# A state-space kernel with an MLP behind it: order of the first loads, of the first differences and of the second weights' decoding

## The chip, the cores and the metric

One Trainium2 chip, one core of it. The metric is device microseconds (us) of one execution, lower is better. A core has a matmul engine (PE), three engines for everything else on chip data (VectorE = DVE, ScalarE = ACT, GpSimd = POOL), a queue processor (SP) that issues DMAs, and 16 DMA engines. Each engine runs its own list of instructions in order and waits on semaphores that others raise; ACT can issue DMAs from its list too (its queue is written ACTq, SP's is SPq).

## The reference, cut to what matters

Two blocks, the second fed by the first. Shapes: 4 batches, 8 heads, 768 steps, head size 32, state size 16.

```python
# block 1, per batch and head, in chunks of the sequence
log_a = np.log(np.clip(a, 1e-6, 1.0)); cum = np.cumsum(log_a of the chunk)
L  = np.exp(cum[:, None] - cum[None, :]) * causal
y  = ((C @ B.T) * L) @ x  +  (C @ state) * np.exp(cum)[:, None]
state = np.exp(cum[-1]) * state + (B * np.exp(cum[-1] - cum)[:, None]).T @ x
# block 2, on 3072 rows (batch x step) of 256 (head x size)
h = y @ w_in                       # 256 -> 2048
g = h * np.clip(h + 3, 0, 6) / 6
out = g @ w_out                    # 2048 -> 256
```

`w_in` and `w_out` come as float64. The kernel takes each weight's halves apart with integer operations and puts a float32 together ("decoding").

## The kernel before, in words

The 768 steps are cut into 6 chunks (c = 0 to 5) of 128 steps. A chunk first gets its block-1 output y, for all 32 pairs of batch and head, and then runs through the MLP as k = c: 16 slices f of the hidden size, each with a matmul into PSUM (`mlp_in` for k = 0), a ramp on ACT (`ramp`, L796) and a product on DVE (`times_ramp`, L801). While the MLP of chunk k runs on PE, the other engines prepare chunk k + 1. The order of all instructions on each engine is the order in which the Python calls them: it is written out by hand at the end of the function. Only chunk 0 has no MLP to hide behind. What follows is its path, which the change rebuilds.

**Loads.** SP issues, in this order: `a` (L83), C of chunk 0 in eight pieces (`pairs_first`, L103, one per batch and half of the heads, 128 rows of 256 bytes each), x (`load_x`, L121, 4096 runs of 128 bytes) and the weight pieces 1 to 3 (`load_w`, L144, 1 MB each). ACT issues weight piece 0 (L144) and B (L96, 4096 runs of 64 bytes), and only then loads its function table (L150). The framework gives the DMAs eight semaphores in turn; a DMA whose semaphore is still in use by an earlier one waits at the head of its queue until that one has landed. By the built program the sixth C piece waits for weight piece 0 in this way, the seventh for `a`, the eighth for the first C piece.

**Decays.** DVE and ACT make log a and its running sum (`log_a` L284 and L286, `add_up` L289), `in_three` (L296 to L300) splits it into three bf16 parts. PE makes the differences cum[i] - cum[j] in a PSUM bank: a mask (`diff_mask`, L370, and `mask_again`, L378), minus the row's sum (`diff_less`, L383, one matmul of 512 columns), plus the column's sum (`diff_pick`). The last has two forms: sixteen narrow matmuls, one per head and half (L399), for batches 0 and 1 of half c = 0; for the rest two matmuls of 512 columns (L391) from a table that DVE spreads by head beforehand (`spread_rows`, L279). `diff_exp` (L407) takes the exponential on ACT into L. Thirty matmuls of one column (L365) stand among the masks. The index c = 0 or 1 here means chunk 0 or 1: both chunks' differences are made in front.

**Scores and output of chunk 0.** `turn_b` turns B with PE (L464) and copies it to SBUF with ACT (L473). `turn_squares` turns C on DVE (L507), `part_heads` makes two masked copies (L517). `busy` (L535) is two matmuls whose result nobody reads. `scores` (L572) makes C times B in four banks; inside it, `into_state` (L590) makes the two half-chunk sums for the state, from x and from B times L's last column (`ends`, on POOL, L438). `multiply` copies one sum (`take`, L606), scales the other (L616) and multiplies L by the scores, pair of heads by pair (L621). `mix` (L667 with `from_state`, L545) makes y, `keep` (L683) copies it to `yT`.

**Weights.** `decode(i)` is a Python generator; `weights(i, n)` advances it n steps, and each step puts a few instructions on ACT (a copy of the top halfword L202, two ramps L227 and L230) and on DVE (L207, L211, L221, L223, L234, L244). Pieces 0 to 3 are w_in, each serves four slices f; pieces 4 to 7 are w_out. Three raw buffers go round. `load_w` of piece 2 is held back by a one-element memset on DVE (L143), since SP must wait for it. Piece 1 is decoded between `mix` and the first slice of the MLP, pieces 2 to 5 are woven into the loop over f (dictionary `weave`). `renew(0)`, which makes the state after chunk 0 (L642, L600), is called behind that loop, among the first products with w_out (`first_out`, L814).

Of the kernel before, what the change touches and what calls it, by code (L numbers as in the profile page):

```python
# [8 lines left out]
FP32 = mybir.dt.float32  # L9
# [12 lines left out]
def kernel(  # L22
# [65 lines left out]
    def load_bc(c):  # L88

        sl = slice(c * P, (c + 1) * P)

        def tokens_first(src, queue=nc.sync, **where):
            t = loads.tile([P, NB * NH, N], FP32, **where)
            queue.dma_start(out=t, in_=src[:, :, sl, :].rearrange("b h s n -> s (b h) n"))  # L96
            return t

        def pairs_first(src):
            t = loads.tile([P, 2, NB, 4, N], FP32, name="pairs", tag="bc")  # L100
            for b in range(NB):
                for h in range(2):
                    nc.sync.dma_start(  # L103
                        out=t[:, h, b].rearrange("s a n -> s (a n)"),
                        in_=src[b, h:NH:2, sl, :].rearrange("h (s a) n -> h s (a n)", a=4))
            return t

        if 0 < c < TURN:
            bcs[c] = [tokens_first(C, name="C", tag="bc")]
        Bs[c] = tokens_first(B, nc.scalar if c == 0 else nc.sync, name="B", bufs=1)  # L110
        if c == 0:
            bcs[c] = [pairs_first(C), Bs[c]]
# [17 lines left out]
    def load_w(i, queue=nc.sync):  # L130
# [57 lines left out]
    parity = const.tile([P, 2], FP32, name="parity")  # L188

    def decode(i):  # L190

# [8 lines left out]
        m = att.tile([P, n], U32, name="wm")  # L200
        for sl in (slice(0, n),) if i != 1 else (slice(0, n // 2), slice(n // 2, n)):
            nc.scalar.copy(out=s[:, sl], in_=top[:, sl])  # L202
            if i == 1 and sl.start == 0:
                yield

# [11 lines left out]
        if i == 0:  # L217
            next(parts_m)
            next(parts_m)
        yield  # L220
# [3 lines left out]
            out=s, in0=s, scalar1=0x8000, scalar2=None, op0=ALU.bitwise_and)  # L224
        next(parts_m, None)
        yield
# [3 lines left out]
        nc.scalar.activation(e, e.bitcast(BF16), AF.Relu, bias=bias_lo, scale=-1.0)  # L230
        if i and i + NRAW < 2 * NP:
            load_w(i + NRAW)
# [21 lines left out]
    low = pre[:G, 10, :2 * P]  # L254
    spread = [pre[:, 11 + c].bitcast(BF16).rearrange("k (h i) -> k h i", h=NH) for c in range(2)]
    of_batch = const.tile([P, NB], BF16, name="of_batch")
    of_head = const.tile([P, NH], BF16, name="of_head")

# [3 lines left out]
    def row_signs():  # L262
        with nc.allow_low_precision("zeros and ones"):
            nc.vector.tensor_reduce(
                out=pick, in_=ident[:, :pad].rearrange("g (r q) -> g q r", r=3), axis=AX.X,
                op=ALU.add)
            nc.vector.tensor_reduce(
                out=of_batch, in_=pick.rearrange("k (b h) -> k b h", b=NB), axis=AX.X, op=ALU.add)
            nc.vector.tensor_reduce(
                out=of_head, in_=pick.rearrange("k (b h) -> k h b", b=NB), axis=AX.X, op=ALU.add)  # L270
        nc.scalar.mul(less, pick, -1.0)
# [3 lines left out]
            out=parity, in_=head.rearrange("p q t -> p t q"), axis=AX.X, op=ALU.add)  # L275

    def spread_rows(c):

        nc.vector.tensor_tensor(  # L279
            out=spread[c], in0=split[:, c].unsqueeze(1).to_broadcast([P, NH, P]),  # L280
            in1=of_head.unsqueeze(2).to_broadcast([P, NH, P]), op=ALU.mult)

# [72 lines left out]
    def diff_mask(c, b):  # L355
# [5 lines left out]
        else:  # L361
            d = ps_y.tile([P, NH, HT], FP32, name="d", tag=f"y{b % 2}")
        if (c, b) == (0, NB - 1):
            for _ in range(30):
                nc.tensor.matmul(  # L365
                    out=d[:1, 0, :1], lhsT=ident_h[:, :1], rhs=hide[:, :1], start=True, stop=True,
                    skip_group_check=True)
        n = NH // 4
        for h in range(0, NH, n):
# [18 lines left out]
    def diff_pick(c, b):  # L388
        if c or b >= 2:
            for a, rows in enumerate(HALF):  # L390
                nc.tensor.matmul(  # L391
                    out=ds[c, b][rows], lhsT=of_batch[:, b:b + 1].to_broadcast([P, HT]),
                    rhs=spread[c][:, :, rows], start=False, stop=True,
                    tile_position=(0, a * HT), skip_group_check=True)
            return
        for h in range(NH):
# [134 lines left out]

    def busy(n, bank):

        for _ in range(n):
            nc.tensor.matmul(  # L535
                out=bank[:, :256], lhsT=ident,
                rhs=ident.unsqueeze(1).to_broadcast([P, 2, P]), start=True, stop=True)

    def from_state(c, a, pairs=range(NQ)):
# [18 lines left out]
    def scores(c):  # L558
# [6 lines left out]
        cbs[c] = [ps.tile([P, NB, 2, HT], FP32, name="cb", tag=f"f{q}") for q in range(NQ)]  # L565
        if c not in ys:
            own_banks(c)
# [8 lines left out]
        if c == TURN:  # L576
            from_state(c, 0)
        if c <= TURN:
            into_state(c, *range(1 if c == TURN else 2))
# [28 lines left out]
    def multiply(c):  # L608
# [579 lines left out]
    for k in range(NC):  # L1188
        gTs[k] = ffn.tile([P, NF, TB], FP32, name="gT")
        c, ahead = k + 1, k + 2  # L1190
        if k == 0:
# [20 lines left out]
            for i in range(NP):  # L1212
                for b in range(NB):
                    first_out(b, i, c)
                    for n in w_more.get((i, b), ()):
                        next(ins[n])
                    if (i, b) == (1, 0):
                        renew(0)
                    if (i, b) == (1, 1):
# [167 lines left out]
```

## Time and profile before

| | |
|---|---|
| time, median of 3 runs (lowest to highest) | 337.47 us (336.9 to 337.77) |
| the profiled execution's own time | 337.3 us |
| its span in the profile | 335.6 us |
| PE busy in the span | 98% |
| DVE, ACT, POOL busy | 79%, 62%, 39% |
| first matmul of the MLP (L693) starts | 21.73 us |
| the 16 slices of k = 0 end on PE | 49.55 us |

The span is the time from the first to the last recorded instruction; 1.7 us of the execution's own time lie around it. A row of a timeline gives start, time taken, engine, line, operation, output <- input, shapes and count; in square brackets stands the idle time of the engine ahead of it and what ended that. The chain of waits is followed back from the last instruction; a piece of it named "issue" is time in which the engine waited for nothing that the profile shows. The table of windows gives, for each stretch, the busy time of each engine with its count of instructions, the clock that the throttle granted to PE, the mean busy share of the DMA engines (it can pass 1) and the bytes moved.

### The profile page before, as it was taken

To read this page: it belongs to the slowest core of one execution; us is meant where nothing else is said; L and a number is where in the kernel's file an instruction comes from. 1 tells how busy PE (TensorE), PEld (TensorE's weight loads), DVE (VectorE), ACT (ScalarE), POOL (GpSimd) and SP (SyncE) were. 2 spreads that over 40 slices of the span, in tenths; PEclk is the share of its full clock that TensorE was granted. 3 is DMA by queue.
4 is the path that set the end of the run, shared out by engine and by line. 5 is a ranking of instruction groups with operands and counts; after the bars stand their busy time and mean duration, and the time that the engine had idled before them with its cause. 6 is when DMAs were issued, how large, how long until landed. Compare 5 with 4: busy or idle time off the path is not lost.

```text
span 335.6 us, 8329 instructions
## 1 busy us (share of the span) xinstructions
PE 327.6 (98%) x3361; PEld 272.8 (81%) x3361; DVE 264.2 (79%) x418; ACT 208.2 (62%) x448; POOL 130.3 (39%) x125
## 2 busy tenths in 40 slices
PE   7989999999999999999999999999999999999995
PEld 5554888888888888887888888888888888899995
DVE  6879999879599639869949558938678958599973
ACT  4778887657987570677662577643487221677661
POOL 2200000280743896089973078771058740000000
PEclk9999999999999999999999999999999999999999
DMA  8979960684930214239107258100151001210001
GB/s 174 158 275 212 215 237 9 154 107 126 197 37 4 60 48 109 41 51 96 42 2 163 35 76 77 33 4 11 28 75 14 2 4 17 29 20 0 2 0 63
DMA packets 90181, 25.22 MB, mean 75 GB/s; under 512 B 82784, under 2 KB 86528, under 8 KB 89632
## 3 DMA queue, kind: packets, MB, share of 16 engines
q1 hardware_dynamic: 85760, 23.39, 36.9%
q10 hardware_dynamic: 4384, 1.31, 1.8%
q8 instruction: 26, 0.43, 0.5%
q14 instruction: 11, 0.09, 0.1%
HBM read 21.33 MB, written 3.29 MB: 73 GB/s over the span
## 4 chain that ended last, share of the span: by engine, by line
PE 90%; DVE 4%; DMA 3%; issue 1%; SPq 1%; ACT 1%; DVEq 0%
PE h L757 31%; PE wc L1005 8%; PE wb L1005 8%; PE o L814 8%; PE h L693 8%; PE wa L1005 7%; PE o_end L969 6%; PE wb L1013 3%; PE y L667 3%; PE y L545 2%; DVE q_part L897 2%; DMA raw<-in_moe_w_in_dram 2%; PE cb L572 2%; DVE gT L801 1%; DMA pairs<-in_C_dram 1%
## 5 line engine op out<-in xcount | busy, mean ns | idle before, releaser
L801 DVE SCALAR_TENSOR_TENSOR gT<-gT,h 128x512 f32<-128x512 f32 x96 | 64.7, 683 | 22.0 <-ACT gT L796 20.7
L796 ACT ACTIVATE gT<-h,half 128x512 f32<-128x512 f32 x96 | 65.5, 684 | 24.3 <-PE h L757 21.1
L777 ACT ACTIVATE h<-h 128x512 f32<-128x512 f32 x66 | 38.3, 585 | 37.0 <-PE h L757 36.7
L757 PE MATMUL h<-y_hi,w_part 128*128 128x512 f32 x160 | 50.9, 403 | 0.0
L757 PE MATMUL h<-y_less,w_part 128*128 128x512 f32 x160 | 50.1, 399 | 0.0
L757 PE MATMUL h<-y_lo,w_part 128*128 128x512 f32 x160 | 49.5, 395 | 0.0
L860 POOL TENSOR_TENSOR s<-gT 128x512 f32<-128x512 f32 x16 | 25.3, 1582 | 51.5 <-DVE gT L801 51.5
L757 PEld LDWEIGHTS h<-y_lo,w_part 128*128 128x128 f32 x160 | 30.0, 188 | 6.9
L757 PEld LDWEIGHTS h<-y_hi,w_part 128*128 128x128 f32 x160 | 30.1, 188 | 6.7
L757 PEld LDWEIGHTS h<-y_less,w_part 128*128 128x128 f32 x160 | 29.1, 188 | 6.2 <-DVE h L774 0.3
L427 ACT ACTIVATE L<-L,cum_n 128x64 f32<-128x64 f32 x128 | 31.7, 337 | 1.8 <-POOL L L162 1.8
L814 PE MATMUL o<-w_out,gT 128*128 128x256 f32 x128 | 28.8, 381 | 0.0
L693 PE MATMUL h<-yT,w_in 128*128 128x256 f32 (+1 forms) x100 | 27.8, 440 | 0.0
L814 PEld LDWEIGHTS o<-w_out,gT 128*128 128x128 f32 x128 | 24.1, 190 | 3.4
L693 PEld LDWEIGHTS h<-yT,w_in 128*128 128x128 f32 x100 | 18.9, 190 | 8.6 <-issue 5.7
L860 POOL TENSOR_TENSOR gT<-gT 128x512 f32<-128x512 f32 x16 | 23.9, 1500 | 0.7
L897 DVE TENSOR_TENSOR q_part<-gT,q_part 128x256 fp32r<-128x256 f32 x24 | 21.5, 923 | 0.1
L969 PE MATMUL o_end<-v_pair,g_pair 128*128 128x256 f32 x120 | 21.1, 281 | 0.0
L346 POOL TENSOR_SCALAR cum_n<-cum_t 128x128 f32<-128x128 f32 x1 | 0.5, 534 | 51.9 <-DVE cum_t L344 51.9
L162 POOL TENSOR_SCALAR_AFFINE_SELECT L<-L 64x1024 f32<-64x1024 f32 (+1 forms) x16 | 19.2, 1210 | 3.5 <-DMA L<-cum_d 3.1
L860 POOL TENSOR_TENSOR s<-s,gT 128x512 f32<-128x512 f32 x16 | 20.6, 1292 | 0.0
L438 POOL TENSOR_TENSOR bs<-B,L 128x128 f32<-128x128 f32 x24 | 12.1, 528 | 21.7 <-ACT L L427 14.2
(163 smaller groups left out, 636.2 us busy)
## 6 DMA issues: line engine op xcount, KB each, us to landing
raw<-in_moe_w_out_dram SPq DMA_DIRECT2D x4, 1024.0 KB
L<-cum_d SPq DMA_DIRECT2D x8, 512.0 KB
xt<-in_x_dram SPq DMA_DIRECT2D x6, 512.0 KB
raw<-in_moe_w_in_dram SPq DMA_DIRECT2D x3, 1024.0 KB
out_dram<-back SPq DMA_DIRECT2D x128, 16.0 KB
pairs<-in_C_dram SPq DMA_DIRECT2D x40, 32.0 KB
B<-in_B_dram SPq DMA_DIRECT2D x5, 256.0 KB
eto<-cum_e SPq DMA_DIRECT2D x20, 64.0 KB
```

The lines of the kernel that those rows point to most:

```text
L162: nc.gpsimd.affine_select(out=t[rows], in_=t[rows], pattern=pattern, compare_op=ALU.is_ge, fill=-1e5, base=base, channel_multiplier=-1)
L427: nc.scalar.activation(Ls[c][:, b, h], Ls[c][:, b, h], AF.Exp, bias=cum_n[:, c, g:g + 1])
L693: nc.tensor.matmul(out=h[:, t:t + n], lhsT=w_in[f // FP][:, j, f % FP * P:(f % FP + 1) * P], rhs=yTs[k][:, j].rearrange("p b i -> p (b i)" ...
L757: nc.tensor.matmul(out=hs_[k, f], lhsT=w[j][:, f % FP * P:(f % FP + 1) * P], rhs=y[:, j], start=(start and j == 0), stop=True, skip_group_ ...
L777: nc.scalar.activation(h, h, AF.Copy, scale=1.0 / EPS + 1.0)
L796: nc.scalar.activation(gTs[k][:, f], h, AF.Relu, bias=half, scale=1.0 / 6.0)
L801: nc.vector.scalar_tensor_tensor(out=g, in0=g, scalar=1.0, in1=h, op0=ALU.min, op1=ALU.mult)
L814: nc.tensor.matmul(out=o[:, b % 2], lhsT=gTs[0][:, f, b * P:(b + 1) * P], rhs=w_out[:, f], start=(f == 0 and b % 2 == 0), stop=True, skip_ ...
L860: nc.gpsimd.tensor_tensor(out=o, in0=p_, in1=q_, op=op)
L897: nc.vector.tensor_tensor(out=l[:, j], in0=g[:, j], in1=h[:, j].bitcast(FP32), op=ALU.subtract)
L969: nc.tensor.matmul(out=ends_["cross" if n == 2 else "squares"][b], lhsT=g_parts[t][n][:, b * P:(b + 1) * P], rhs=w, start=(t == 0 and b < ...
L1005: nc.tensor.matmul(out=bank[:, slot], lhsT=lhs[:, j], rhs=rhs[:, j], start=(clear and j == 0), stop=True, skip_group_check=True)
```

## The change

- SP's queue: the eight C pieces are cut by head (32 rows by 4 batches of 256 bytes) and not by batch and half of the heads. B follows them on SP, then x. ACT loads its function table first and then issues weight piece 0. By the built program, the seventh C piece waits for `a`, the eighth for the first C piece, and B waits for weight piece 0.
- Weight piece 1 is no longer issued in front. A memset on DVE behind the first product of `multiply(0)` holds it, as another held piece 2 before.
- `spread_rows`, `of_batch`, `of_head` and the wide form of `diff_pick` are gone: every head's difference is made by its own narrow matmuls, for both chunks. The thirty one-column matmuls and `busy` are gone, and the masks are wider (256 or 512 columns and not 128).
- PE's order: differences of chunk 0, those of batch 0 and 1 of chunk 1 around the turning of B, scores, then the differences of batches 2 and 3 of chunk 1 with their exponentials, and only then `into_state`, which has been taken out of `scores`.
- `turn_squares(C)` and `part_heads` move to the front of DVE's list, right behind `in_three`; B's turned copy is made by DVE and not by ACT.
- `decode(0)` takes its second significand step later; `decode(1)` is replaced by `decode_halves(1)`, which runs whole behind `keep(0)`, the exponent part in two halves of the columns. `renew(0)` is called in front of `mix(0)`.
- `mlp_in` runs every matmul 512 columns wide; before, the last 18 of 32 were two of 256.

```diff
-            for b in range(NB):
-                for h in range(2): ... in_=src[b, h:NH:2, sl, :] "h (s a) n -> h s (a n)"
+            if c == 0:
+                for h in range(NH):
+                    rows = slice(h // 2 * 32, h // 2 * 32 + 32)
+                    nc.sync.dma_start(
+                        out=t[rows, h % 2].rearrange("s b a n -> s b (a n)"),
+                        in_=src[:, h, sl, :].rearrange("b (s a) n -> s b (a n)", a=4))
+                return t
...
-        Bs[c] = tokens_first(B, nc.scalar if c == 0 else nc.sync, name="B", bufs=1)
+        Bs[c] = tokens_first(B, name="B", bufs=1)      # behind pairs_first(C)
...
-        if i == 2:
+        if 0 < i < 3:
             nc.vector.memset(raw[:, :1], 0)
...
-    load_w(0, nc.scalar)
-    load_bc(0)
-    load_x(0)
-    load_w(1)
-    nc.scalar.preload_act_table_set("natural_log_exp_and_others")
+    load_bc(0)
+    nc.scalar.preload_act_table_set("natural_log_exp_and_others")
+    load_w(0, nc.scalar)
+    load_x(0)
...
+    def decode_halves(i):
+        for h in halves:
+            nc.scalar.copy(out=s[:, :, h], in_=top[:, :, h])
+        nc.vector.tensor_scalar(out=m, in0=hi, ...)                    # 128x1024
+        for h in halves:
+            for t, mask in ((e, 0x7FF0), (s, 0x8000)):
+                nc.vector.tensor_scalar(out=t[:, :, h], in0=s[:, :, h], ...)
+            nc.scalar.activation(e[:, :, h].bitcast(BF16), e[:, :, h], AF.Relu, ...)
+            nc.scalar.activation(e[:, :, h], e[:, :, h].bitcast(BF16), AF.Relu, ...)
+        nc.vector.scalar_tensor_tensor(out=m.bitcast(FP32), in0=lo, ...)   # 128x1024
+        load_w(i + NRAW)
+        for h in halves:
+            nc.vector.tensor_tensor(out=e[:, :, h], ...)
+            nc.vector.scalar_tensor_tensor(out=w_in[i][:, :, h], ...)
...
-        nc.scalar.copy(out=turned(c)[0], in_=t_ps)
+        (nc.scalar.copy if c else nc.vector.tensor_copy)(out=turned(c)[0], in_=t_ps)
...
+            if c == 0 and q == 0:
+                load_w(1)                              # in multiply
...
-            n = TB // (1 + (f * NK + j >= NF * NK - 18))
+            n = TB // (1 + (f * NK + j >= NF * NK - 0))
...
-    for c in range(2):
-        spread_rows(c)
-    diff(0, 0, 1)
-    diff(0, 2, 3)
+    turn_squares(bcs[0][0], turned(0)[2])
+    part_heads(0)
     weights(0, 1)
+    for b in (0, 2):
+        diff(0, b, b + 1)
     for b in range(NB):
         diff_exp(0, b)
     first_eto()
-    diff(1, 2, 3)
     weights(0, 1)
+    diff(1, 0)
+    turn_b(0)
+    diff(1, 1)
     for b in range(NB):
         ends(0, b)
-    turn_b(0)
-    diff(1, 0, 1)
-    weights(0, 2)
-    diff_exp(1, 2)
-    diff_exp(1, 3)
-    turn_squares(bcs[0][0], turned(0)[2])
-    part_heads(0)
+    weights(0, 1)
+    scores(0)
+    weights(0, 1)
+    for b in range(2, NB):
+        diff(1, b)
+        diff_exp(1, b)
+    own_banks(0)
+    into_state(0, 0, 1)
+    multiply(0)
     fade(0, HALF[1])
     weights(0, 1)
-    busy(2, ps.tile([P, NB * P], FP32, name="d", tag="f3"))
-    scores(0)
-    multiply(0)
+    weights(0, 1)
     load_w(2)
     load_w(3)
-    weights(0, 1)
-    weights(1, 1)
+    renew(0)
     mix(0)
-    keep(0, lambda: weights(1, 1))
-    weights(1, 3)
-    weights(1, 1)
+    keep(0)
+    decode_halves(1)
```

More of the change, by code (lines that the diff above doesn't have):

```diff
@@ L109, in load_bc @@
             bcs[c] = [tokens_first(C, name="C", tag="bc")]
-        Bs[c] = tokens_first(B, nc.scalar if c == 0 else nc.sync, name="B", bufs=1)
         if c == 0:
-            bcs[c] = [pairs_first(C), Bs[c]]
+            bcs[c] = [pairs_first(C)]
+        Bs[c] = tokens_first(B, name="B", bufs=1)
+        if c == 0:
+            bcs[c].append(Bs[c])
         elif c < TURN:
@@ L188 @@
     parity = const.tile([P, 2], FP32, name="parity")
+    def decode_halves(i):
+        n, cut = NK * FP * P, FP * P // 2
+        top = raws[i].bitcast(U16).rearrange("p (k f w) -> p k f w", k=NK, w=4)[..., 3]
+        lo, hi = (raws[i].rearrange("p (n w) -> p n w", w=2)[:, :, w] for w in range(2))
+        s = att.tile([P, n], U16, name="ws").rearrange("p (k f) -> p k f", k=NK)
+        e = att.tile([P, n], U16, name="we").rearrange("p (k f) -> p k f", k=NK)
+        m = att.tile([P, n], U32, name="wm")
+        halves = [slice(h * cut, (h + 1) * cut) for h in range(2)]
+        for h in halves:
+            nc.scalar.copy(out=s[:, :, h], in_=top[:, :, h])
+        nc.vector.tensor_scalar(
+            out=m, in0=hi, scalar1=0xFFFFF, scalar2=0x100000,
+            op0=ALU.bitwise_and, op1=ALU.bitwise_or)
+        for h in halves:
+            for t, mask in ((e, 0x7FF0), (s, 0x8000)):
+                nc.vector.tensor_scalar(
+                    out=t[:, :, h], in0=s[:, :, h], scalar1=mask, scalar2=None,
+                    op0=ALU.bitwise_and)
+            nc.scalar.activation(
+                e[:, :, h].bitcast(BF16), e[:, :, h], AF.Relu, bias=bias_hi, scale=-8.0)
+            nc.scalar.activation(
+                e[:, :, h], e[:, :, h].bitcast(BF16), AF.Relu, bias=bias_lo, scale=-1.0)
+        nc.vector.scalar_tensor_tensor(
+            out=m.bitcast(FP32), in0=lo, scalar=2.0 ** -32, in1=m, op0=ALU.mult, op1=ALU.add)
+        load_w(i + NRAW)
+        m = m.bitcast(FP32).rearrange("p (k f) -> p k f", k=NK)
+        for h in halves:
+            nc.vector.tensor_tensor(
+                out=e[:, :, h], in0=e[:, :, h], in1=s[:, :, h], op=ALU.bitwise_or)
+            nc.vector.scalar_tensor_tensor(
+                out=w_in[i][:, :, h], in0=m[:, :, h], scalar=2.0 ** -20,
+                in1=e[:, :, h].bitcast(BF16), op0=ALU.mult, op1=ALU.mult)
     def decode(i):
@@ L200, in decode @@
         m = att.tile([P, n], U32, name="wm")
[L201 to L204, printed above, removed]
+        nc.scalar.copy(out=s, in_=top)
         def significand():
@@ L218, in decode @@
             next(parts_m)
-            next(parts_m)
         yield
@@ L224, in decode @@
             out=s, in0=s, scalar1=0x8000, scalar2=None, op0=ALU.bitwise_and)
-        next(parts_m, None)
+        if i:
+            next(parts_m)
         yield
@@ L230, in decode @@
         nc.scalar.activation(e, e.bitcast(BF16), AF.Relu, bias=bias_lo, scale=-1.0)
-        if i and i + NRAW < 2 * NP:
+        if i > 1 and i + NRAW < 2 * NP:
             load_w(i + NRAW)
@@ L254 @@
     low = pre[:G, 10, :2 * P]
-    spread = [pre[:, 11 + c].bitcast(BF16).rearrange("k (h i) -> k h i", h=NH) for c in range(2)]
-    of_batch = const.tile([P, NB], BF16, name="of_batch")
-    of_head = const.tile([P, NH], BF16, name="of_head")
     cum_c = cum.rearrange("g (c p) -> g c p", p=P)
@@ L266, in row_signs @@
                 op=ALU.add)
[L267 to L270, printed above, removed]
         nc.scalar.mul(less, pick, -1.0)
@@ L275, in row_signs @@
             out=parity, in_=head.rearrange("p q t -> p t q"), axis=AX.X, op=ALU.add)
[L277 to L281, printed above, removed]
     def log_a(sl):
@@ L362, in diff_mask @@
             d = ps_y.tile([P, NH, HT], FP32, name="d", tag=f"y{b % 2}")
[L363 to L368, printed above, removed]
+        n = NH if c else NH // (2 if b == 0 else 4)
         for h in range(0, NH, n):
@@ L388, in diff_pick @@
     def diff_pick(c, b):
[L389 to L395, printed above, removed]
         for h in range(NH):
@@ L530, in turn_all @@
         fade(c)
[L532 to L537, printed above, removed]
     def from_state(c, a, pairs=range(NQ)):
@@ L565, in scores @@
         cbs[c] = [ps.tile([P, NB, 2, HT], FP32, name="cb", tag=f"f{q}") for q in range(NQ)]
-        if c not in ys:
+        if c not in ys and c:
             own_banks(c)
@@ L577, in scores @@
             from_state(c, 0)
-        if c <= TURN:
+        if 0 < c <= TURN:
             into_state(c, *range(1 if c == TURN else 2))
@@ L1216 @@
                         next(ins[n])
-                    if (i, b) == (1, 0):
-                        renew(0)
                     if (i, b) == (1, 1):
```

## The prediction, made before the changed kernel ran

> **What bounds the kernel now.** I read the chain of waits first. From 21.80 us on it is PE almost without a break: the MLP of chunk 0, then the products with w_out (L814). So a gain must come from an earlier start of that stretch, or from PE needing less inside it. Second, the chain's first 22 us:
>
> ```profile
> 0.79 6.00 DMA raw<-in_moe_w_in_dram
> 6.80 0.71 SPq L103
> ...
> 7.56 1.58 SPq L103
> ...
> 9.18 3.62 DMA pairs<-in_C_dram
> ...
> 12.98 1.12 DVE csT L507
> ...
> 15.16 1.20 PE cb L572 x59
> 16.36 0.84 PE y L590 x50
> ...
> 17.22 0.38 ACT adds L606
> ...
> 17.64 0.90 PE y L667 x55
> ...
> 19.42 1.03 issue
> 20.44 0.75 PE y L667 x43
> ```
>
> The reader sees C arriving last: its sixth piece waits for weight piece 0 to land (6.80), the eighth lands at 12.80. Everything behind is a chain of single steps, with one hole of 1.03 us (19.42) that no semaphore explains. Third, the table of windows:
>
> ```profile
> 4.00:5.00 1.00, 1.00 (x23) 0.97 (x19) 0.83 (x3) 0.66 (x2) 0.00 (x0) 1.00 1.01 393
> 9.00:10.00 1.00, 1.00 (x34) 0.54 (x28) 1.00 (x2) 0.68 (x2) 0.00 (x0) 1.00 0.40 70
> ```
>
> The last two columns say that weight piece 0 moved at 393 GB/s, but that while C is the latest thing the DMA engines were 40% busy at 70 GB/s. The packet records of the trace agree: C's 256-byte packets take 18 ns, some 60 to 90 start per half microsecond, and their times add up to 2 to 4 busy engines of 16. Fourth, the waits of DVE, ACT and PE: from 25.21 to 65 us DVE is never idle, so DVE is the second bound of k = 0.
>
> **Part 1, arrival of C and B.** SP issues a C piece in 0.59 to 0.71 us when nothing holds it, so eight from 1.25 end at about 6.1. Spread evenly, a piece is 8 packets per engine (0.15 us). The record from issue to use of a small load is that of `a`: issued 0.79, used 4.02; the packets of weight pieces start 0.5 to 1.2 us behind the issue. I take C at 8.0 (bounds: 7.3, if the last piece needs only 1.2 us behind its issue; 9.3, if SP is held up as in its 2.14 us piece at 4.55).
>
> [...]
>
> Weight piece 0 goes behind the table load (L150, 1.28 us), so issue near 2.1 and not 0.79. It took 6.0 us from issue to landing beside `a`, whose cold packets held the engines until about 3; with those past I take 4.9, that is 7.0 (5.9 if the DMA isn't held by the table load, 8.0 at the old 6.0). B waits for it on SP: issue 0.5 us, first packet 0.4 us later, 4096 packets in 2.3 us (second B load, packets 32.0 to 34.3), 0.4 us to land: 10.7 (bounds 9.6 and 12.2). Before, B was used at 10.9. x follows: its packets took 4.2 us before (11.0 to 15.3), now 10.4 to 14.5.
>
> **Part 2, from B and C to the MLP.** C's arm on DVE: turn 1.12 and masked copies 0.89, then three decoding steps (L207 0.69, L221 and L223 0.43 each) stand ahead of B's copy: 8.0 + 0.2 + 3.56 = 11.8. B's arm: 10.7 + 0.66 (L464) = 11.4. B's copy on DVE is not in the trace; its neighbours are ACT's 0.59 (L473) and a DVE product from the same bank, 0.69 (L489): 0.65, ends 12.45. Scores 1.20: 13.7, against 16.36. Now the added wait: differences of batches 2 and 3 of chunk 1 stand between. Each is one matmul of 0.30 (L383, two in 0.60) and sixteen narrow ones (L399, 32 in 0.84: 0.42); two make 1.44, so 15.1. Their exponentials (0.55) follow 0.25 us behind the last matmul and free the banks: 15.95. Behind that wait stands `into_state`, and all of PE. It runs 0.85 (L590): 16.85, not 17.19. x is there (14.9), POOL's four products (2.32 from 10.7) end at 13.0. ACT's copy opens `mix` as before, 0.45 us later: 17.3, not 17.64. L's products on DVE (4 x 0.62 from 13.9) end at 16.4 and the fade at 16.85, so the second half of `mix`, which no longer meets a late DVE, isn't held. From `mix` to the MLP the trace has 21.73 - 17.64 = 4.09 with the hole of 1.03 in it.
>
> **The hole.** It stands behind some 705 instructions on PE, and the instruction queue's packets (26 of 16 KB, so 256 instructions of 64 bytes each) start at 9.78, 18.19, 24.40. The second started only when weight piece 1 had left the engines (its packets 14.5 to 18.1) and ended 1.28 us ahead of the matmul at 20.44. I read it as a late fetch of the third block. After the change PE passes the place where that fetch was asked for (some 320 instructions earlier, the end of scores) at 13.6, and weight piece 1 is issued only behind the first product, at 14.6. So the fetch goes out first: 14.4 to 15.4, usable at 16.7, needed at 18.1. The hole goes; the MLP starts at 17.3 + 3.06 = 20.35, which is 1.38 us earlier. Bounds: no hole, or all of it and more (rival 2).
>
> [...]
>
> **Part 3, inside k = 0.** Matmul width: 72 of 256 columns took 15.7 us; 36 of 512 at 0.429 take 15.4: -0.27. Weight piece 1 lands at about 18.7 (issue 14.6, packets 3.1, start and landing 1.0), as before (18.70), and is used when ACT is done with `yT`, 0.5 us into the MLP. Halves cost about half of a whole row (ACT copy 0.66 as measured; ramps 0.6 of 1.15; DVE 0.22 of 0.43, 0.35 of 0.69, 0.61 of 1.22). ACT: two copies and four ramps end 4.2 us into the MLP; DVE ends 5.4 in (4.7 before), and w_in[1]'s first half is there at 4.4, needed at 6.86. But ACT's first ramp of the MLP comes at 4.2 (2.6 before), the second at 5.9, so DVE's products slip: the fourth slice's bank is free 13.4 us into the MLP, and PE wants it at 13.75. Cover left: 0.35 us, where the trace had 1.7. Then it holds, as DVE needs 6.8 us for four slices and a decoding (33.14 to 39.94) and PE 6.86. I charge nothing; bounds 0 and +0.8 (two whole ramps more than reckoned, beyond the cover). `renew(0)` (0.42 and 0.61) moves from DVE's full stretch at 63.8 to a place where DVE waits for weights: nothing. Removed DVE work (2.36 and 0.39 us) lay beside waits: nothing. The 96 more narrow matmuls are counted above or lie ahead of B's landing.
>
> **Sum.** -1.38 - 0.27 = -1.65 us. Against the profiled execution's 337.3 that is 335.65; the median shown lies 0.17 above it. I forecast **335.7**. A measurement of this kernel tells about 0.3% (1.0 us) from no change.
>
> **Rivals.** (1) *The gain is half eaten on the way*: C or B later (C at 9.3 makes B's copy wait for DVE and costs 1.1, B at 12.2 costs 0.9 to 1.5), or DVE becomes the bound of k = 0 (+0.8). For it: thin covers (0.35 us; two arms of one length). Against: no single row demands it. Time: 336.4 to 337.2. Chance 0.28.
>
> (2) *The fetch stays late.* If the request comes 1 us later than I read it, it meets weight piece 1 on the engines (15.0 to 18.1) and is usable at 20.4, as before. Then PE still has 0.13 + 0.61 + 0.84 + 0.61 us to do: MLP at 22.6, +0.9 - 0.27: 337.9. If the hole has another cause and stays as it is (MLP at 21.38): 336.7. Chance 0.10 for both.
>
> (3) *PE stays slow, slower than before.* Matmuls of 512 columns are 0.43 us apart until 8.5 us (L378: three in 1.49) and 0.22 from 9.5 on (L383: two in 0.60), at a granted clock of 1.00 throughout, so PE's speed doubles only after 6.4 us of unbroken matmuls. The change takes the fillers out: masks are 4.7 us (2.1 to 6.8), then PE waits some 0.5 us for `split`. If the doubling needs that unbroken stretch anew, the 3.3 us of difference work ahead of B's turn run at half speed: it ends at 13 to 13.9 and not 10.7, and the MLP starts 2.2 to 3.2 us later, at 22.6 to 23.5. With -0.27, 337.9 to 338.9; if scores are slow too (+1.2), 340. It decides once PE's wait at 6.8 counts as a break. Against: before, breaks of 0.61 and 1.03 us (14.45, 19.42) left the speed as it was. Chance 0.14.
>
> [...]
>
> (4) *It doesn't do what it says.* If ACT's DMA isn't held by the table load, C's first pieces wait behind weight piece 0 until 5.6, as before, and its packets still end near 7: the forecast's time. If the C pieces stay on some 3.3 engines, 1024 packets of 18 ns take 5.6 us and C lands near 9.5: B's copy is 1.3 us later, which is rival 1.
>
> **How the numbers follow.** Forecast 0.48 (335.2 to 336.3), rival 1 0.28, rival 2 0.10, rival 3 0.14. Range 334.9 to 338.3: rivals 1 and 2 whole, rival 3's lower end. Faster by over 0.3% (below 336.4) is the forecast and a little of rival 1: 0.50; slower by over 0.3% (above 338.4) is the upper part of rival 3: 0.10; the rest 0.40.
>
> **What would show it.** C's turn on DVE starts near 8 (12.98 before); scores near 12.5; `into_state` only 0.3 us earlier; no hole in `mix`; first L693 (now L702) near 20.3; PE without idle in k = 0. An idle PE there, ended by DVE, is rival 1; an "issue" wait in `mix` rival 2; matmuls 0.43 us apart behind 9 us rival 3.

## The result, and the profile after

The changed kernel takes 346.94 us (median of 4 executions, 344.62 to 347.63) against 337.19 us (4 executions, 336.75 to 337.77) for the kernel before on the same chip: a ratio of 1.0276, 95% interval 1.0222 to 1.033. It is slower, where 335.7 was forecast, and outside the range. The profiled execution took 344.62 us, its span is 342.9 us. (Ratios leave out executions over 1.5% above a kernel's fastest; medians hold all.)

The chain of waits of the kernel after, from C's arrival to the MLP (start, time taken, what):

```profile
1.25 5.76 DMA pairs<-in_C_dram
7.03 0.31 SPq L104
...
7.38 4.93 DMA B<-in_B_dram
...
12.44 0.64 PE t_ps L478 x4
...
13.11 0.70 DVE bT L487
...
13.94 1.20 PE cb L579 x60
...
16.52 0.74 issue
17.26 0.86 PE y L597 x50
18.15 0.38 ACT adds L613
...
18.57 0.79 PE y L676 x49
19.36 3.28 issue
22.64 0.44 PE y L676 x8
...
26.28 30.46 PE h L702 x64
```

C no longer ends the first stretch, B does. Scores start at 13.94 (15.16 before), so 1.2 us were won there. Then `into_state` starts at 17.26 (16.36 before), and the gap in `mix` without a semaphore is 3.28 us long where it was 1.03. The MLP starts 4.5 us later, and its 64 matmuls take 30.46 us. The table of windows shows why they are slow (last three columns: PE's clock, DMA share, GB/s):

```profile
18.00:20.00 2.00, 0.90 (x67) 0.63 (x57) 1.97 (x5) 0.90 (x3) 0.00 (x0) 1.00 0.91 365
20.00:22.00 2.00, 0.00 (x0) 0.00 (x0) 1.53 (x4) 0.00 (x0) 0.00 (x0) 0.91 0.73 162
22.00:24.00 2.00, 1.36 (x24) 1.12 (x23) 0.01 (x1) 0.37 (x1) 0.00 (x0) 0.50 0.90 340
...
28.00:30.00 2.00, 2.00 (x4) 0.89 (x3) 1.93 (x5) 1.94 (x4) 0.00 (x0) 0.50 0.06 16
...
32.00:34.00 2.00, 2.00 (x6) 0.93 (x5) 0.86 (x2) 0.81 (x2) 0.00 (x0) 1.00 0.86 336
```

PE stands still from 19.36 to 22.64 us, while weight piece 1 moves (packets 16.95 to 20.78; 365 GB/s in the first row). Then the clock is 0.50, and the matmuls of the MLP start 0.85 us apart and not 0.43. The clock's records put this at 21.64 to 31.88, three times 3.41 us. Before, the clock was 1.00 from 9.07 us on.

The loss up to the first product with w_out (49.55 us before, 56.74 after: +7.19) therefore has four parts: `mix` starts 0.93 later (18.57 against 17.64); the gap is 2.25 longer; the rest of `mix` takes 4.36 instead of 3.06 at the half clock, +1.30; the MLP takes 30.53 instead of 27.82, +2.71. From there on both traces run in step: +7.25 at chunk 2, +7.31 at the end.

### The profile page after: what moved, and what is told of

It is laid out like the page before. It is cut to its first block, busy times and chain, and to the rows that moved or that the text cites. A ratio compares the mean times of both kernels' runs of the same rounds, so it can differ in the third digit from the quotient of the medians.

```text
span 342.9 us, 8334 instructions
## 1 busy us (share of the span) xinstructions
PE 330.5 (96%) x3361; PEld 266.3 (78%) x3361; DVE 262.7 (77%) x420; ACT 208.7 (61%) x449; POOL 128.5 (37%) x125
## 4 chain that ended last, share of the span: by engine, by line
PE 89%; DVE 4%; DMA 3%; issue 2%; ACT 1%; SPq 0%; DVEq 0%
PE h L766 31%; PE h L702 9%; PE wc L1014 8%; PE o L823 8%; PE wb L1014 8%; PE wa L1014 7%; PE o_end L978 6%; PE y L676 3%; PE wb L1022 3%; PE y L552 2%; DVE q_part L906 2%; DMA pairs<-in_C_dram 2%; PE cb L579 2%; DMA B<-in_B_dram 1%; DVE gT L810 1%
## 5 line engine op out<-in xcount | busy, mean ns | idle before, releaser
L702 PE MATMUL h<-yT,w_in 128*128 128x512 f32 x64 | 30.5, 642 | 0.0
L702 PEld LDWEIGHTS h<-yT,w_in 128*128 128x128 f32 x64 | 13.2, 208 | 16.7 <-issue 15.3
L978 PEld LDWEIGHTS o_end<-v_pair,g_pair 128*128 128x128 f32 x120 | 18.8, 189 | 1.2
```

Source lines behind the costliest of these rows:

```text
L702: nc.tensor.matmul(out=h[:, t:t + n], lhsT=w_in[f // FP][:, j, f % FP * P:(f % FP + 1) * P], rhs=yTs[k][:, j].rearrange("p b i -> p (b i)" ...
L978: nc.tensor.matmul(out=ends_["cross" if n == 2 else "squares"][b], lhsT=g_parts[t][n][:, b * P:(b + 1) * P], rhs=w, start=(t == 0 and b < ...
```

## The experiments

Three theories stood at the start. **A**: PE's instructions come in blocks of 256, the gap is a block that comes late, and the half clock follows from PE's idle time. **B**: something else holds PE (the removed idle matmuls, the order of C, B and x, the arithmetic of the differences). **C**: DVE and ACT are late inside k = 0. The kernel after's own trace speaks against C: from the start of the MLP to 60 us PE has no wait over 0.15 us. Positions below count the PE records of the trace (matmuls, weight loads and a few others, 6752 of them in both kernels). The gap in `mix` lies at position 705 in both. (The trace names no semaphore for a second wait of the kernel after either, 0.74 us ahead of `into_state`; it ends at 17.26, just behind the exponentials on ACT, 17.17, which Part 2 of the prediction has it wait for.) In the kernel before the instruction queue moved 26 packets of 16 KB for these 6752 records, some 260 to a packet:

```profile
q8 instruction: 26, 0.43, 0.5%
```

**1. When weight piece 1 moves.** First, piece 1 held until behind the fade:

```diff
-            if c == 0 and q == 0:
-                load_w(1)              # in multiply
...
     fade(0, HALF[1])
+    load_w(1)
```

> The changed kernel, with the hold of weight piece 1 moved behind the fade, some 2 us later on DVE; PE's instructions are the same. Theory A (PE's third block of instructions is fetched behind weight piece 1, PE stands 3.3 us, then its clock halves): the fetch starts before weight piece 1 does, no hole in mix, clock 1.00 from 9 us on, MLP starts at 21.6 us, 336.4 to 337.5 us. Theory B (the clock falls since the filler matmuls are gone): clock 0.5 in part again, 340 us or more. Theory C (DVE and ACT are late inside k = 0): 344 us or more.

Measured: 343.55 us (340.47 to 347.69), ratio 1.0141 [1.0024, 1.0258]. Its chain:

```profile
18.53 0.79 PE y L674 x49
19.32 1.38 issue
20.70 0.32 PE y L674 x8
```

The gap shrinks from 3.28 to 1.38 us with nothing but the weight piece moved: its packets now start at 19.05, the instruction packet at 18.28 (20.38 in the kernel after). But it doesn't vanish, the clock is still 0.50 from 21.32 to 28.15, and the time misses A's 336.4 to 337.5 by 6 us. Second, piece 1 not held at all, issued right behind x:

```diff
-        if 0 < i < 3:
+        if i == 2:
...
     load_x(0)
+    load_w(1)
...
-            if c == 0 and q == 0:
-                load_w(1)              # in multiply
```

> The changed kernel, with weight piece 1 issued in front, right behind x, as before the change. Theory A: its packets run from 15 to 18.3 us, the fetch starts when they end, usable at 20.5 us: a hole of about 1.1 us in mix, too short to halve the clock; MLP at 22.8 us, 337.5 to 338.5 us. Theory B: 340 us or more. Theory C: 344 us or more.

Measured: 342.74 us (340.38 to 343.78), ratio 1.0126 [1.0058, 1.0194]. The expected time was missed by 5 us, for a reason that I had not priced. The waits of PE:

```profile
PE t_ps L479 <- DMA B<-in_B_dram: 3.9, 1, 3.9
...
PE y L675 <- issue: 1.3, 1, 1.3
```

B comes 2 us later still, the clock falls during that wait (12.42 to 19.24) and again behind the gap. The gap is 1.29 us, again far below 3.28: no weights move when the instruction packet starts (21.90).

**2. Where the block ends.** Thirty one-column matmuls, narrow masks and two idle matmuls back in the kernel after; then, instead, the wide form of the differences of chunk 1 (112 PE instructions fewer):

```diff
+            for _ in range(30): nc.tensor.matmul(out=d[:1, 0, :1], ...)
-        n = NH if c else NH // (2 if b == 0 else 4)
+        n = NH // 4
...
+    busy(2, ...)                       # ahead of scores
```

> The changed kernel with the thirty one-column matmuls, the narrow masks and the two filler matmuls ahead of scores put back. Theory A: the hole stays at 3 us or more and comes some 90 instructions earlier in PE's order, at the start of mix; the clock halves again; 344 to 348 us. Theory B: the clock stays at 1.00, 340 us or less.

```diff
     def diff_pick(c, b):
+        if c:
+            for a, rows in enumerate(HALF):
+                nc.tensor.matmul(out=ds[c, b][rows], lhsT=of_batch..., rhs=spread[c]...)
+            return
...                                     # and spread_rows(1) on DVE, ahead of turn_squares
```

> The changed kernel with chunk 1's differences in the wide form (one more DVE step of 1.2 us in front, 112 fewer instructions on PE). Theory A: the hole moves 112 instructions later, into the second half of mix, and is about 2.5 us long, since weight piece 1 still stands ahead of the fetch; 340 to 345 us. Theories B and C: as the changed kernel, hole or not, 344 us or more.

Measured: 355.54 us (ratio 1.0514 [1.042, 1.0609]) and 349.07 us (1.0323 [1.0232, 1.0414]). What B says of the idle matmuls falls: with them back it is worse. A's times were missed too, since I had looked at the first 22 us only. The first one's waits of PE:

```profile
PE y L564 <- issue: 5.5, 4, 1.8
PE y L688 <- issue: 2.3, 1, 2.3
```

There are now gaps in the later chunks as well. Their positions in the two runs are 961, 1985, 3009, 4033, 5057, 6081 and 705, 1473, 2753, 3777, 4801: every one is 193 beyond a multiple of 256. (For the one at 5057, in the first run, the profile names a step of DVE, L924, as what the matmul waited for; the weight load beside it waited for nothing that the profile shows.) I read this as block ends that move with the count of instructions ahead of them and here fell into dense stretches (four of the first run's gaps, 5.5 us in all, stand at L564, among the short matmuls of `from_state`). To test it without the change: the kernel before with only the full-width `mlp_in`, 72 records fewer.

```diff
-            n = TB // (1 + (f * NK + j >= NF * NK - 18))
+            n = TB // (1 + (f * NK + j >= NF * NK - 0))
```

> The kernel before with mlp_in at full width only: 72 PE instructions fewer in all of k = 0, nothing else moved. Prediction's reading (width alone): 0.27 us faster, 336.9 to 337.4. Theory A (PE's list arrives in blocks of 256 instructions; where a dense stretch of a chunk crosses a block's end, PE waits without a semaphore): the ends of the blocks behind k = 0 now fall 72 instructions later in every later chunk, as in the run with the wide differences, so gaps of 1 to 2 us appear at PE's instructions 193 beyond a multiple of 256, in some of the chunks 1 to 5; 340 to 346 us. The first 22 us are as before (gap of 1.03 at instruction 705).

Measured: 342.71 us (342.19, 343.22), ratio 1.0158 [1.0134, 1.0182], as A expected. The waits of PE and, in chunk 1, the rows of its timeline:

```profile
PE y L667 <- issue: 3.9, 3, 1.9
...
PE y L590 <- issue: 1.2, 1, 1.2
```

```profile
72.51 0.74 PE L590 MATMUL y<-xt,bs 64*32 64x64 f32 x50
74.44 0.34 PE L590 MATMUL y<-xt,bs 64*32 64x64 f32 x14 [1.19 <-issue]
```

New gaps stand at 1473, 3777 and 4801 (1.19, 1.91, 1.07 us), three of the positions of the run with the wide differences. k = 0 itself is only 0.09 us shorter (27.66 against 27.75 in the chains), a third of the prediction's 0.27. Then the count put back with idle work:

```diff
-            for _ in range(30):
+            for _ in range(66):
```

> The run e5_phase (kernel before with mlp_in at full width, 72 trace records fewer, 342.71 us) with 36 more one-column matmuls beside the thirty among the first masks, where PE waits anyway: the number of PE instructions behind k = 0 is that of before again. Theory A (block ends): the gaps of e5_phase at instructions 1473, 3777 and 4801 are gone, and what is left is the width's 0.25 us: 336.5 to 337.3 us. In the first 22 us the block end falls 72 instructions earlier in mix, the request for it too, so its gap stays at 0.7 to 1.2 us. Rival (the full width itself disturbs the later chunks, by what it does to VectorE or to the clock): the gaps and 342 to 343 us stay.

Measured: 341.35 us (339.5 to 341.96), ratio 1.0119 [1.008, 1.0159]. Half of A's expectation came true. Behind 70 us PE has no wait any more, and the distance to the kernel before stays at 3.8 to 4.1 us from chunk 1 to the end: the gaps of the later chunks hang on the count alone. The time was missed, because the first 22 us came out worse: with 36 more idle matmuls `into_state` starts at 17.32 (16.36 before), the gap at 705 is 1.62 us and two windows of half clock follow (20.44 to 27.27).

**3. The loads and C alone, in the kernel before.**

```diff
+            if c == 0:                 # C by head, as in the change
...
-        Bs[c] = tokens_first(B, nc.scalar if c == 0 else nc.sync, ...)
+        Bs[c] = tokens_first(B, ...)   # behind C
...
-    load_w(0, nc.scalar)               # ahead of load_bc(0)
+    nc.scalar.preload_act_table_set("natural_log_exp_and_others")
+    load_w(0, nc.scalar)
```

> The kernel before with the change's loads alone (C by head, B on SP behind C, function table ahead of weight piece 0, piece 1 still issued in front); PE's list untouched. C should land near 8.6 as in the kernel after, but DVE still turns it where it did, so nothing is won by it; B's packets end near 11 and it is usable near 12.3 (10.86 before). Theory A: B's turn is 1.4 us later, but the path of before had C's turn end at 14.1, so scores move from 15.16 to at most 15.5; time 337 to 338.5. Rival (the loads are what cost the 7 us, by way of B): scores 1.4 us later, PE's wait for B pulls the clock down, 340 to 344.

Measured: 338.9 us (337.43 to 341.17, 10 executions), ratio 1.0049 [1.0025, 1.0074], just above A's 337 to 338.5. The loads cost little in themselves: with a mean clock of 0.998 to 1.000 single executions took 337.4 to 339.3 us, with 0.995 or less 340.0 to 341.2. In the profiled one (341.17) PE waits 1.55 us for B, and two windows of half clock begin at 21.54.

```diff
+            if c == 0:                 # C by head
...
-    for c in range(2):
-        spread_rows(c)
+    spread_rows(0)
+    turn_squares(bcs[0][0], turned(0)[2])
+    spread_rows(1)
+    part_heads(0)
...                                     # busy: 16 columns, not 256
```

> The kernel before with only C by head and its turn and masked copies early on DVE, and the two idle matmuls of busy narrowed to 16 columns; weight piece 0 and B on ACT's queue as before, piece 1 issued in front, same number of PE instructions. Theory A: scores start near 13.4 (15.16), into_state and mix 1.5 us earlier than before; the block with instruction 705 comes later relative to them, so the gap grows from 1.03 to 1.5 to 2.2; MLP at 20.6 to 21.4 (21.73): 336.3 to 337. Rival (the gap is tied to weight traffic, which is over by then): gap under 0.5, MLP at 19.7 to 20.2, 335.2 to 335.9.

Measured: 342.18 us (340.67 to 343.59), ratio 1.0142 [1.01, 1.0183]. The expectation was missed because the edit made a wait of its own:

```profile
PE d L398 <- DVE pre L286: 3.0, 1, 3.0
```

C's turn on DVE stood ahead of the second `spread_rows`, PE waited 3 us for that, and the clock fell from 14.92 to 21.74. Scores took 2.05 us and `into_state` 1.19 at the half clock (1.20 and 0.84 before), so PE came to position 705 later, and the gap there is only 0.48 us; so this run doesn't answer the question on the gap.

**4. The order of the differences.** All differences of chunk 1 and their two exponentials ahead of B's turn, first with piece 1 held behind the fade:

```diff
-    diff(1, 0)
-    turn_b(0)
-    diff(1, 1)
+    for b in range(NB):
+        diff(1, b)
+    for b in range(2, NB):
+        diff_exp(1, b)
+    turn_b(0)
...
     weights(0, 1)
-    for b in range(2, NB):
-        diff(1, b)
-        diff_exp(1, b)
     own_banks(0)
...                                     # and load_w(1) behind fade
```

> The kernel after with all differences of chunk 1 and their exponentials ahead of B's turn (they fill PE's wait for B, and no wait stands between scores and into_state), and weight piece 1 held back until behind the fade. Same number of PE instructions. Theory A: into_state starts near 15.2 and mix near 16.6 (18.57 in after); instruction 705 cannot be there before some 4 us behind instruction 449, so a gap of 1.5 to 2.5 us stays in mix; the MLP starts at 21 to 22. If the clock stays at 1.0: 336 to 337.5 us; if one or two windows of half clock remain: 338.5 to 341. Rival (the gap comes from weight traffic alone): no gap, MLP at 20 to 20.5, 335 to 336.5.

Measured: 341.42 us (340.46 to 343.71), ratio 1.013 [1.009, 1.0169]. The MLP starts at 20.71, 1.02 us earlier than in the kernel before, and there is no gap in `mix`. A's expectation failed here (it had a gap of 1.5 to 2.5 us stay): position 705 ran 3.40 us behind 449, and not 4. What is left is a price of my own edit:

```profile
PE h L700 <- DVE gT L808: 3.2, 1, 3.2
```

The fifth slice of the MLP waits for weight piece 1, which came too late; a half-clock window follows that (32.25 to 35.66). So the same order with the piece where the change has it:

> The kernel after with one edit only: all differences of chunk 1 and the two exponentials stand ahead of B's turn, as in the run e7_order; weight piece 1 is held where the kernel after holds it (behind the first product of multiply). Theory A (PE's next 256 instructions are asked for when it passes instruction 449, here near 15.0, and go out before the weight piece if that is issued later): the request goes out at 15.9 as in e7_order, weight piece 1 follows at 17 to 21, no gap over 0.3 us in mix, MLP at 20.7 and no wait for weight piece 1 at its fifth slice (3.21 us in e7_order): 335.5 to 337 us, with up to 2 us more in executions in which a window of half clock falls in. Rival (the gap in after comes from the weight piece whatever the order): a gap of 2 us or more comes back in mix, MLP at 22.5 or later, 338 to 341.

Measured: 338.76 us (336.9 to 342.58, 12 executions), ratio 1.0043 [1.002, 1.0066]. Against the changed kernel one edit of order takes 8 us off (338.76 against 346.94; the kernel before took 336.77 on this chip and 337.19 on that one). Its chain, and two windows:

```profile
16.35 1.19 PE y L597 x58
...
17.99 1.18 PE y L676 x63
19.17 1.04 PE y L552 x16
20.21 1.11 PE y L676 x61
21.33 1.05 PE y L552 x16
22.37 7.86 PE h L702 x13
```

```profile
18.00:20.00 2.00, 2.00 (x80) 1.83 (x80) 1.97 (x5) 0.84 (x3) 0.00 (x0) 0.50 0.93 379
...
24.00:26.00 2.00, 2.00 (x4) 0.80 (x3) 1.97 (x4) 1.94 (x4) 0.00 (x0) 0.50 1.01 412
```

No gap, though weight piece 1 moves at 379 GB/s all through `mix`: the instruction packet had started at 15.47, before the piece (16.94). The rival (the piece makes the gap whatever the order) falls, though a run below has the same order and a gap. The clock is 0.50 from 16.29 to 26.53 in this execution (340.15 us), and the MLP starts at 22.3; with the clock at 1.00 there the run before had 20.71.

**5. Keeping the clock up.** The same with idle matmuls in PE's waits for B's copy and for x:

```diff
+    busy(2, ...)                       # ahead of scores, 256 columns each
     scores(0)
...
     own_banks(0)
+    busy(2, ...)                       # ahead of into_state
```

> The run e9_both with four idle matmuls of 256 columns: two in PE's wait for the copy of B's turn (0.77 us), two in its wait for x (1.12 us); four mask matmuls fewer (two pairs joined into one each), so that the number of PE instructions stays. Theory A (the clock falls to half for whole 3.41 us windows when PE stood still too much in the window before; in e9_both executions at full clock took 336.9 to 337.3 us and those with half clock up to 342.6): the clock stays at 1.00 from 10 us on, all executions lie within 1 us of one another, MLP at 20.7 to 20.9, 336 to 337. Rival (the half clock has another cause, such as load or the chip's state): the spread of 336.9 to 342.6 us and the median of 338.8 stay.

Measured: 338.29 us (336.76 to 342.61, 12 executions), ratio 1.0034 [1.0017, 1.005]. In the profiled execution (337.72 us) the clock is 1.00 throughout and the MLP starts at 20.74; eleven of the twelve executions have a mean clock of 0.998 to 1.000 (336.76 to 339.66 us), the twelfth 0.988 (342.61); in the run without the idle matmuls it was seven of twelve. That is too few to tell what the idle matmuls do (the next two builds, which have them too, come to six and five of twelve), and the spread did not close to 1 us. PE's waits show what is next:

```profile
PE h L709 <- DVE gT L817: 0.5, 1, 0.5
...
PE wb L1029 <- issue: 0.3, 1, 0.3
```

PE now waits for VectorE inside k = 0, so that of the 1.0 us won at the start of the MLP 0.31 are left at the first product with w_out. The second line is a block end again (position 5057): this build has 8 records more. The next two have 6752 again, the second with piece 1 released one product earlier:

> The run e11_warm with one idle matmul of 512 columns and one of 256 in place of four of 256, so that the trace has exactly as many PE instructions as before and after (6752 with the weight loads; e11_warm had 6760 and a gap of 0.32 us at one of its block ends in chunk 4). Theory A: no gaps at block ends in chunks 1 to 5, clock mostly 1.00; but PE waits for VectorE in k = 0 (0.48 us in e11_warm), so that about 0.3 to 0.7 us of the earlier MLP are left: 336.3 to 337.3 us, executions closer together than in e11_warm. Rival (the spread of e11_warm, 336.8 to 339.7, came from something else than those 8 instructions): the same spread and a median near 338.

> The run e13_even with weight piece 1 released ahead of the first product of multiply and not behind it, 1.0 us earlier (packets from about 16.3). Theory A: if the instruction request (about 15.9) still goes out first, piece 1 and 2 are decoded 0.5 to 1 us earlier and PE's wait for VectorE in k = 0 shrinks: 0.3 to 0.5 us less than e13_even, 336 to 336.8. If the request falls behind the first packets of the piece, a gap of 1 us or more opens in mix: 337.5 to 339.

Measured: 340.44 us (336.82 to 345.14), ratio 1.0057 [1.0024, 1.009], and 340.87 us (336.98 to 344.06), ratio 1.0034 [1.0003, 1.0065], 12 executions each. Both expectations on the time failed, and most of the reason stands in the clock. In the second kernel five executions have a mean clock of 0.998 to 1.000 and took 336.98 to 337.42 us; two at 0.995 took 340.7 and 341.04; those at 0.990 took 342.62 and 342.79, one at 0.988 took 342.98, and two at 0.984 took 343.26 and 344.06. One window of 3.41 us at half clock is 0.005 of the span, so these are about 0, 1, 2 and 3 windows. (In the run with the order and piece 1 late the times do not follow the clock so: 340.46 at 0.985, 341.71 at 0.994.) Why the clock fell oftener here than in the run before (its second stretch of idle matmuls was twice as long) isn't settled. In the profiled execution of the first a gap of 1.89 us came back and two windows followed:

```profile
PE y L682 <- issue: 1.9, 1, 1.9
```

Its instruction packet starts at 17.73, in the same instant as piece 1, and takes 1.70 us (0.95 in the kernel after). In the second kernel's profiled execution neither came. No version beat the kernel before.

## Why the prediction was wrong, point by point

**The step that failed is "The hole".** It said that the third block is asked for "some 320 instructions earlier, the end of scores", at 13.6, and so "goes out first: 14.4 to 15.4, usable at 16.7". In the kernel after the packet started at 20.38, when weight piece 1 was nearly through, and the block was used at 22.64. The times, each of the profiled execution (449 is the record 256 ahead of 705):

| run | PE passes 449 | instruction packet starts | 705 runs | gap before it |
|---|---|---|---|---|
| before | 16.53 | 18.19 | 20.44 | 1.03 |
| after | 16.23 | 20.38 | 22.64 | 3.28 |
| piece 1 late | 16.19 | 18.28 | 20.70 | 1.38 |
| piece 1 early | 19.87 | 21.90 | 24.30 | 1.29 |
| order, piece 1 late | 15.05 | 15.88 | 18.45 | none |
| order alone | 14.71 | 15.47 | 18.73 | none |
| order and idle matmuls | 15.21 | 15.99 | 18.47 | none |
| the same, with 6752 records | 15.53 | 17.73 | 20.69 | 1.89 |
| that, with piece 1 earliest | 15.18 | 16.06 | 18.74 | none |
| before, full width, 36 more one-column matmuls | 16.22 | 18.45 | 21.03 | 1.62 |

From packet to use it takes 2.25 and 2.26 us in the two kernels. From 449 to the packet it takes 0.5 to 0.9 us in six of the fifteen traces; 1.3 to 1.7 in four whose piece 1 is just ending then, the kernel before among them (packets to 18.14, instruction packet 18.19); 2.0 to 2.2 in another four; 4.15 in the kernel after. No run passed these 256 records in less than 3.26 us.

So the order of the two loads is what the prediction had wrong. The packet did not start by 15.4 but was still out when piece 1 began (packets 16.95 to 20.78). With the piece moved away and all else as it was, it started at 18.28 and the gap fell from 3.28 to 1.38; with the exponentials of chunk 1 out of PE's way too it started at 15.88 and there was no gap. That is rival 2's mechanism ("it meets weight piece 1 on the engines"), which I had given 0.10 and 337.9 us, and whose consequence for the clock I had not seen. One part is plain: PE passed the place that I had reckoned with, position 385, at 14.76 and not 13.6, since B came late.

When the request goes out is not shown. It isn't PE's passing of 449: in the MLP, where PE needs long for each record, packets start up to 9 us before PE enters the block (29.94 against 38.98 in the kernel after). Over the later blocks of all fifteen traces none starts before the record 44 ahead of the block's first has run. What the four traces with 2.0 to 2.2 us share is that the packet came 0.99 to 1.13 us behind a wait of PE ahead of `into_state`, at positions 462 and 463 (`into_state` started at 17.22 with piece 1 late, at 20.91 with piece 1 early, at 16.70 and 17.32 in the other two). In the changed kernel that is the wait for the exponentials, which the change itself put there. But in other runs with a wait at 462 the packet started before `into_state` did (order alone: 15.48 against 16.35), so it is no rule, and it was not isolated.

That a block holds 256 instructions is read from the positions of the gaps, all 193 beyond a multiple of 256 in the run with the idle matmuls back and the one with the wide differences; a packet of 16 KB then has 64 bytes for each. The "some 320 instructions earlier" was my estimate, and no run shows a place at which a block is asked for. In the ten runs of the table, the end of the block at 705 cost between nothing and 3.28 us.

**The clock.** Rival 3 named the half clock, but at the start, from the masks; there it stayed away. Its reading of the start ("at a granted clock of 1.00 throughout") was wrong: the kernel before's clock records begin at 9.07 us, the view prints 1.00 for what lies ahead of them, and the matmuls of 512 columns are 0.43 us apart up to 8.5 and 0.22 from 9.5 on. In the kernel after the records begin at 7.98, and the matmuls of 512 columns are 0.40 us apart at 7.04 and 0.23 at 8.63. So the matmuls' spacing halves where the records of the full clock begin, 1.1 us earlier than before and not later.

The half clock came later. I cut the fifteen profiled executions into windows of 3.41 us on the clock's own edges, from the first record on, without the last 10 us, in which PE runs out of work. Fourteen windows had PE busy for half of the time or less (0.23 in the kernel after); behind thirteen of them the clock was 0.50. Behind one, in the kernel before with the full width, it stayed at 1.00:

```profile
175.23:178.65 3.42, 1.51 (x151) 1.35 (x148) 1.03 (x3) 0.62 (x2) 1.52 (x4) 1.00 0.02 5
```

Behind none over 0.62 did a full clock fall (the kernel before has 0.70 at its lowest); between 0.53 and 0.62 both happened. It then lasts one to three windows (3.41, 6.83 or 10.24 us), though PE is mostly busy in them. That it is PE's standstill, and not the load on the DMA engines, is argued from these windows; the runs with idle matmuls do not settle it, and it wasn't isolated. The same build ends on either side in different executions (the order alone has a mean clock of 0.998 to 1.000 in seven of twelve). Counted from the span's start, the clock's edges differ from trace to trace: modulo 10.24 / 3 us, at 2.24 in the kernel before, 1.15 after, 0.84 with piece 1 late, 2.64 with the order alone.

In the kernel after the half clock held for three windows (21.64 to 31.88): PE was busy for 2.41 us of the first, and throughout the other two (3.42 and 3.41 us).

**Part 1.** C: right. Landed by the start of its turn on DVE, at 8.72 (8.0 forecast, 7.3 to 9.3):

```profile
8.72 1.11 DVE L521 STREAM_TRANSPOSE csT<-pairs 128x512 f32<-128x512 f32 x1 [1.73 <-DMA pairs<-in_C_dram]
```

That a piece is spread evenly over the 16 engines, from which its 0.15 us came, was my estimate, and the trace of before doesn't show it. In the kernel after the times of C's packets add up to 11 engines at work from 5.5 to 6.0 us and 20 from 6.0 to 6.5 (the sum can pass 16), against 2 to 5 before (6.0 to 12.0 us).

"Issue near 2.1" behind the table load: wrong. ACT issues the weights beside its table load, as rival 4 had it (and C's packets started at 5.51, as the weights ended):

```profile
0.78 1.28 ACT L156 ACT_TABLE_LOAD   x1 [0.78 <-PEq L1378]
0.81 0.48 ACTq L153 DMA_DIRECT2D raw<-in_moe_w_in_dram  x1
```

Of C in the kernel before, "some 60 to 90 start per half microsecond" was read low at the end: from 10.5 to 11.5 us it was 140.

B: mis-sized. Used at 12.31 and not 10.7, just beyond the bound of 12.2. Its last packet starts at 10.95 (10.3 by my sum; the issue alone was 0.38 later), and "0.4 us to land" was 1.36 us: 0.65 and 0.96 make the 1.6.

**Part 2.** B's copy on VectorE: 0.69 to 0.70 (0.65). The added differences: 1.38 us (1.44), the wait for their exponentials 0.74 (0.85). So `mix` at 18.57 and not 17.3 is B's error of 1.6 less a little that was reckoned too dear. The sign of this term turned by B alone: -0.34 forecast, +0.93 measured.

**Part 3.** Width: mis-sized. Seen alone it is worth -0.09 and not -0.27: in the kernel before the 72 narrow matmuls take 15.54 us (15.7 in the prediction), the 36 wide ones 15.45. And that holds only as long as the count of PE instructions doesn't shift; in the changed kernel the other edits happen to restore the 72 records (3361 matmuls in both). By itself the same edit costs 5.6 us. I had not asked for the count at all. "Cover left: 0.35 us": too thin to hold once the MLP starts early. With the gap and the clock cured PE waits 0.48 us for VectorE (rival 1), and in the run with piece 1 earliest the MLP is 0.74 us ahead, still 0.82 ahead at the first product with w_out, 0.32 at chunk 2, and 0.12 behind at the end, with no wait of PE over 0.2 us behind the MLP's start; where the rest goes isn't settled.

**The sum.** -1.38 - 0.27 was to be -1.65; the first stretch came to +4.5 at the start of the MLP, and the half clock took another 2.7 inside k = 0. The nearest to the idea without gap and half clock is the profiled execution with order and idle matmuls: the MLP 1.0 us earlier, and the time (337.72) not below the kernel before.

## What to carry to other kernels

Before instructions are added to, or taken from, an engine that is the bound, count them: 72 PE records less put gaps of 1.07 to 1.91 us into `into_state` and `mix` of later chunks here, and cost 5.6 us with no work added. Look for the instruction packets in the trace before placing a large load: a weight load that went out ahead of one made a gap of 3.28 us, the same load behind it 1.38. And price an idle stretch of PE at more than its length: 3.28 us of standstill took another 4 us by the half clock that followed.

## What the hardware showed that I had not expected

- Apart from the wait ahead of `into_state`, the gaps without a semaphore on PE stood at positions 193 beyond a multiple of 256 in the three builds with several gaps (15 gaps with the one that the profile puts down to DVE), and they were 0.7 to 2.3 us long.
- B's way from its last packet to its first use was 1.36 us (10.95 to 12.31).
- Cut with 32 rows outermost, C had up to some 450 packets started per half microsecond, against at most 140 before; it was ready at 8.7 and not 12.98 us.
- The DMA that ACT issued did not wait for ACT's table load (0.81 beside 0.78 to 2.06 us).
